# A gated MLP kernel: sums of the plain chunks kept in DRAM instead of in SBUF

## The chip, the cores and the metric

The kernel runs on one core of a Trainium2 chip. The metric is the device time of one execution in microseconds; each version is run several times and the median counts. The profile is of one further execution, which has a time of its own.

## What is computed

One transformer layer on 2048 tokens of width 576, in float32: layernorm, attention of 32 heads in which each token sees 8 tokens at steps of 2, an output projection with a residual, layernorm again, and a gated MLP with a hidden width of 4608.

```python
x = A_x
h = x + _A_ref(_layernorm(x), A_wqkv, A_wo)          # attention over 8 positions, then wo
g = einsum("bsd,df->bsf", layernorm(h), w_gate)
u = einsum("bsd,df->bsf", layernorm(h), w_up)
h2 = h + einsum("bsf,fd->bsd", sigmoid(g) * u, w_down)
```

## The kernel before

**Blocks and precision.** The tokens lie in four blocks of 512 (`BLOCKS`). Matrix products are made in float32 accuracy from halves: `split` (L103 to L105) has ScalarE write the rounded upper part of an operand (L104) and VectorE the remainder (L105), and three matmuls take the place of one. So each operand, whether a weight, an activation or a hidden value, costs one ScalarE and one VectorE instruction.

**Stages.** First come layernorm, the q, k and v projections and part of attention (to about 225 us). Then the MLP goes through its 4608 hidden columns in chunks of 128 (`F`, `NF` = 36), in a list of items (L1123) that is also the order of the program:

- twelve plain chunks (`NSTD` = 12) for block 0 (about 225 to 365 us),
- 24 paired chunks for blocks 0 and 1 together (to about 806 us),
- twelve plain chunks for block 1 (to about 950 us),
- 36 paired chunks for blocks 2 and 3 (to the end).

A paired chunk computes two blocks with seven products in place of eight (`pair`, L818); for that the inputs of its two blocks are combined into sums and differences (`sums`, L279 to L291: the rows L281 to L289) and split. A plain chunk (`single`, L783) needs one block only. While plain chunks of block 0 run on TensorE, attention and the output projection of block 1 run in between them (`under_first`, L1033); while plain chunks of block 1 run, the projections of blocks 2 and 3 do (`under_rest`, L1052). These steps in between are handed out at fixed places of a chunk (`bg_step`, L1086).

**Background steps that matter here.** Attention is VectorE's: products, reductions and sums of 128x2304 elements (L189 to L226). A finished group of heads goes out to DRAM by GpSimd's queue (L228, L230), and the projection loads it again by SyncE's queue (L707 in `paced`). It is transposed by TensorE (L146, L150), split (L105, L109), multiplied (L157 to L160), added to the residual by VectorE (L262) and normalised (`ln_j`, L118), where GpSimd computes one power (L126). Weights of a chunk are loaded by L702 into one of two buffers; a buffer is free when ScalarE and VectorE have split what it held.

**The down product.** Every two chunks there is a set of four units per block, one for each 128 tokens. A unit is `down_tile` (L859): twelve matmuls (L868) into a PSUM tile `dp`, of which there are two, and then its emptying, `add_tile` (L873): a copy by ScalarE (L876) or an addition to what lies in SBUF by VectorE (L878). Units stand in a list (`queue`, L1110) and are handed out at fixed places of a chunk (`units`, L1112).

In the paired chunks of blocks 0 and 1, `down_units` (L886) copies four units into a fresh `stage` tile with ScalarE, and `add_dram` (L883) adds the whole tile, 1152 KB, to `hacc[b]` in DRAM with one accumulating transfer of GpSimd's queue (L884). In the paired chunks of blocks 2 and 3, `down_seven` does the same with pieces of 576 and 288 KB (L936, L939). In the plain chunks, `down_std` (L895) keeps one `stage` tile through all six sets of a block: the first set is copied into it, the other five are added by VectorE, and after the sixth the tile is added to `hacc[b]` with one transfer. `hacc[b]` holds the residual from the projection before (L625, L973) and is sent to the output later (L1256).

**What sets the order.** The order of instructions on each engine is fixed when the kernel is built, from the order of the program, from priorities (`tc.high_priority`, the emptying of PSUM with `HC`, splits and projections mostly with `HI`) and from a cost model. On the chip each engine takes its queue in order and waits where an operand isn't there. GpSimd's transfers have the ordinary priority.

Of the kernel before, what the change touches and what calls it, by code (L numbers as in the profile page):

```python
# [18 lines left out]
ALU = mybir.AluOpType  # L19
# [4 lines left out]
D = 576  # L24
# [6 lines left out]
NS = 4  # L31
# [23 lines left out]
NSTD = 12  # L55
# [5 lines left out]
def kernel(ctx, tc, x, wqkv, wo, wmlp, out):  # L61
    nc = tc.nc
    dve, act, pool, pe, sp = nc.vector, nc.scalar, nc.gpsimd, nc.tensor, nc.sync
# [29 lines left out]
    hacc = [dr.tile([P, NS, D], F32, name=f"h{b}") for b in range(2)]  # L93
# [765 lines left out]
    def down_tile(seg, t, j):  # L859
        js = slice(j * P, (j + 1) * P)  # L860
        ps = gp.tile([P, 2, 512], F32, bufs=2, name="dp")
        k = 0
        n = 3 * len(seg) - 1
        for hid, d in seg:
            hh, hl = hid[t]
            for a, m in ((hh, 0), (hl, 0), (hh, 1)):
                for i in range(2):
                    pe.matmul(ps[:, i, :DH2], a[:, js], d[:, m, i * DH2:(i + 1) * DH2],  # L868
                              start=k == 0, stop=k == n)
                k += 1  # L870
        return ps[:, :, :DH2]

    def add_tile(hv, ps, copy):  # L873
        with tc.high_priority(HC):
            if copy:
                act.activation(hv, ps, AF.Copy)  # L876
            else:
                dve.tensor_tensor(hv, hv, ps, ALU.add)  # L878

    def halved(hs, j):  # L880
        return hs[:, j].rearrange("p (i n) -> p i n", i=2)

    def add_dram(b, hs):  # L883
        pool.dma_start(hacc[b], hs, accum_op=ALU.add, max_dma_last_dim=8 * D)  # L884
# [10 lines left out]
    def down_std(seg, b, n):  # L895
        if n == 0:
            tails[b] = st.tile([P, NS, D], F32, name="stage")
        hs = tails[b]
        for j in range(NS):
            add_tile(halved(hs, j), down_tile(seg, b, j), n == 0)  # L900
            if j == NS - 1 and n == NSTD // 2 - 1:
                add_dram(b, hs)
            yield

    def down_tail(seg, b, end):
# [220 lines left out]
    seg = []  # L1126
# [124 lines left out]
    for c, (kind, p, f) in enumerate(items):  # L1251
# [68 lines left out]
        if len(seg) == 2:  # L1320
            if by_seven and f == NF - NPL + 1:
                queue.append(load_tails())
            for b in blocks:
                queue.append(down_std(seg, b, f // 2) if kind == "std" else
                             down_tail(seg, b, f == NF - 1) if by_seven else down_units(seg, b))
            seg = []
# [44 lines left out]
```

## Time and profile before

| | |
|---|---|
| median of 3 runs | 1567.01 us (1566.04 to 1567.74) |
| profiled execution | 1568.13 us, of it 1566.4 us span |
| granted TensorE clock | 0.999 |
| TensorE, weight loads | 1542.5 us, 1373.7 us |
| VectorE | 1253.5 us |
| ScalarE | 874.0 us |
| GpSimd | 207.1 us |
| moved | 273.96 MB, 175 GB/s |

A busy time is the time in which the engine has an instruction of its own at work, and DMA issues count on GpSimd's row as its instructions. Matmuls overlap in a pipeline, so TensorE can be busy in the profile and yet be handed matmuls more slowly than it could take them; the pace at which matmuls start tells that. In rows of a timeline the columns are start, length, engine, line and operation, written tile and read tiles, and behind them, in brackets, the idle time of the engine ahead of the row and what ended it. Engines: PE is TensorE, PEld its weight loads, DVE VectorE, ACT ScalarE, POOL GpSimd, SP SyncE.

### The profile page before, as it was taken

The page shows a single profiled execution, that of the slowest core. Times are in us where ns is not written, and L with a number is a line of the kernel's source. Part 1 is how long each engine was busy: PE and PEld are TensorE (multiplying, and loading weights), DVE is VectorE, ACT ScalarE, POOL GpSimd, SP SyncE. Part 2 cuts the span into 40 slices and gives each one's busy share as a digit, 9 for nine tenths or more (in the row PEclk, how much of TensorE's full clock was granted, in tenths as well). Part 3 has the DMA queues.
Part 4 walks back from the last instruction along what each step waited for, and adds up shares of the span by engine and source line. Part 5 has one row for each costly group of instructions (what it writes and reads, how often), then busy time and mean ns, then how long its engine had stood idle before and what let it go on. Part 6 is the DMA issues. An engine that isn't in the chain of part 4 may idle for free.

```text
span 1566.4 us, 22385 instructions
## 1 busy us (share of the span) xinstructions
PE 1542.5 (98%) x8520; PEld 1373.7 (88%) x8520; DVE 1253.5 (80%) x1880; ACT 874.0 (56%) x1584; POOL 207.1 (13%) x252
## 2 busy tenths in 40 slices
PE   8999999999999999999999999999999999999998
PEld 7899888887888888888888888888888888888888
DVE  6998999969999999999526588866777776677754
ACT  6632245435656555666542355766677766677761
POOL 2300000011000110001101010112121121111212
PEclk9999999999999999999999999999999999999999
DMA  8646545266566776665683424898888889888984
GB/s 279 211 173 211 202 186 192 100 220 212 121 186 167 184 183 160 165 161 117 170 243 128 175 81 127 186 189 177 167 177 190 183 164 191 177 161 187 190 167 136
DMA packets 77148, 273.96 MB, mean 175 GB/s; under 512 B 8336, under 2 KB 14224, under 8 KB 76144
## 3 DMA queue, kind: packets, MB, share of 16 engines
q0 software_dynamic: 28192, 107.29, 37.4%
q1 hardware_dynamic: 41216, 145.11, 27.0%
q10 hardware_dynamic: 7632, 20.12, 3.4%
q8 instruction: 66, 1.08, 0.3%
q14 instruction: 42, 0.34, 0.1%
HBM read 143.98 MB, written 130.87 MB: 175 GB/s over the span
## 4 chain that ended last, share of the span: by engine, by line
PE 83%; DVE 8%; DMA 5%; ACT 1%; issue 1%; POOL 0%; ACTq 0%; SPq 0%; POOLq 0%; DVEq 0%
PE b L747 41%; PE dp L868 15%; PE dp L930 11%; PE b L754 8%; PE acc L157 4%; DMA wg<-in_wmlp_dram 2%; DVE pr L189 1%; DVE lg L193 1%; DVE pr L215 1%; PE b L157 1%; PE bgp L157 1%; DMA kw<-k 1%; DMA x<-tok 1%; DMA k<-ev 1%; DVE w L105 0%
## 5 line engine op out<-in xcount | busy, mean ns | idle before, releaser
L747 PE MATMUL b<-tl,w 128*128 128x512 f32 x1692 | 423.4, 392 | 1.6 <-ACT s L824 1.0
L747 PEld LDWEIGHTS b<-tl,w 128*128 128x128 f32 x1692 | 307.6, 188 | 59.7 <-ACT s L824 1.5
L747 PE MATMUL b<-th,w 128*128 128x512 f32 x1332 | 341.4, 391 | 0.4 <-DVE s L843 0.4
L747 PEld LDWEIGHTS b<-th,w 128*128 128x128 f32 x1332 | 246.0, 188 | 48.9 <-DVE s L843 0.8
L754 PE MATMUL b<-th,w 128*128 128x512 f32 x564 | 174.6, 390 | 0.0
L939 POOL DMA_DIRECT2D h<-ev x128 | 109.2, 853 | 455.9 <-ACT ev L936 451.0
L104 ACT ACTIVATE w<-wg 128x384 fp32r<-128x384 f32 (+1 forms) x186 | 111.0, 600 | 91.2 <-PE b L754 47.3
L157 PE MATMUL acc<-qw,th 128*128 128x432 f32 x512 | 154.3, 362 | 3.1 <-DVE th L109 2.3
L936 ACT ACTIVATE ev<-dp 128x576 f32<-128x576 f32 x224 | 139.0, 648 | 22.0 <-PE dp L930 22.0
L105 DVE TENSOR_TENSOR w<-wg,w 128x384 fp32r<-128x384 f32 (+1 forms) x186 | 120.9, 655 | 37.3 <-ACT w L104 37.1
L105 DVE TENSOR_TENSOR w<-tw,w 128x512 fp32r<-128x512 f32 x120 | 82.5, 688 | 79.6 <-ACT w L104 79.3
L754 PEld LDWEIGHTS b<-th,w 128*128 128x128 f32 x564 | 105.9, 188 | 22.5
L104 ACT ACTIVATE w<-tw 128x512 fp32r<-128x512 f32 x120 | 75.6, 630 | 83.4 <-PE b L747 82.3
L868 PE MATMUL dp<-d,h1h 128*128 128x288 f32 x640 | 118.8, 295 | 0.0
L868 PE MATMUL dp<-d,h0h 128*128 128x288 f32 x608 | 112.3, 295 | 0.0
L876 ACT ACTIVATE stage<-dp 128x576 f32<-128x576 f32 x104 | 66.9, 646 | 68.3 <-PE dp L868 68.1
L157 PEld LDWEIGHTS acc<-qw,th 128*128 128x128 f32 x512 | 96.7, 189 | 8.8 <-DVE th L109 3.4
L868 PEld LDWEIGHTS dp<-d,h1h 128*128 128x128 f32 x640 | 98.8, 189 | 3.0
L868 PEld LDWEIGHTS dp<-d,h0h 128*128 128x128 f32 x608 | 94.0, 189 | 3.5 <-DVE stage L878 0.3
L157 PE MATMUL acc<-qw,tl 128*128 128x432 f32 x256 | 92.8, 362 | 0.1
L189 DVE TENSOR_TENSOR pr<-kw,q 128x2304 f32<-128x2304 f32 x32 | 81.8, 2556 | 10.9 <-DMA kw<-k 10.7
L884 POOL DMA_DIRECT2D h<-stage x26 | 31.1, 1197 | 416.6 <-ACT stage L876 337.6
(323 smaller groups left out, 2971.6 us busy)
## 6 DMA issues: line engine op xcount, KB each, us to landing
h<-ev POOLq DMA_DIRECT2D x96, 576.0 KB, 7.1
wg<-in_wmlp_dram SPq DMA_DIRECT2D x47, 928.0 KB, 5.2
h<-stage POOLq DMA_DIRECT2D x26, 1152.0 KB, 11.7
wg<-in_wmlp_dram SPq DMA_DIRECT2D x36, 640.0 KB, 5.3
kw<-k SPq DMA_DIRECT2D x16, 792.0 KB, 5.1
vw<-v SPq DMA_DIRECT2D x16, 792.0 KB, 5.1
wd<-in_wmlp_dram SPq DMA_DIRECT2D x18, 576.0 KB, 8.1
h<-ev POOLq DMA_DIRECT2D x32, 288.0 KB, 5.1
```

The source lines that it names most:

```text
L104: act.activation(hi, src, AF.Copy)
L105: splits.append(dve.tensor_tensor(lo, src, f32(hi), ALU.subtract))
L157: pe.matmul(ps[:, :n], a[:, c, js], m[:, c], start=k == 0, stop=False)
L189: dve.tensor_tensor(pr, both(kw, u), q[:, us].unsqueeze(2).broadcast_to([P, 2, W, CG]), ALU.mult)
L747: pe.matmul(ps, wt[:, a, k0 + c], xx[:, m + c], start=first and k == 0, stop=k == 5, skip_group_check=True)
L754: pe.matmul(ps, wt[:, a, k0], xx[:, 4], start=False, stop=a == 1, skip_group_check=True)
L868: pe.matmul(ps[:, i, :DH2], a[:, js], d[:, m, i * DH2:(i + 1) * DH2], start=k == 0, stop=k == n)
L876: act.activation(hv, ps, AF.Copy)
L884: pool.dma_start(hacc[b], hs, accum_op=ALU.add, max_dma_last_dim=8 * D)
L930: pe.matmul(ps[:, i, :DH2], a[x][:, js], m[y], start=k in (0, 1, 3) and q == 0, stop=q == 2, skip_group_check=True)
L936: act.activation(hs[:, k % 2], ps[:, :, :DH2], AF.Copy)
L939: pool.dma_start(hsev[:, u, k0:k + 1], hs[:, :k + 1 - k0], accum_op=ALU.add, max_dma_last_dim=8 * D)
```

## The change

In `down_std` all six sets are copied by ScalarE, and each unit's row of the `stage` tile, 288 KB, is added to `hacc[b]` in DRAM right after its copy, by an accumulating transfer of GpSimd's queue. The VectorE addition and the one transfer behind the sixth set are gone. The `stage` tile stays the same through the six sets, so a row is written again in each of them.

```diff
         hs = tails[b]
         for j in range(NS):
-            add_tile(halved(hs, j), down_tile(seg, b, j), n == 0)
-            if j == NS - 1 and n == NSTD // 2 - 1:
-                add_dram(b, hs)
+            add_tile(halved(hs, j), down_tile(seg, b, j), True)
+            pool.dma_start(hacc[b][:, j], hs[:, j], accum_op=ALU.add, max_dma_last_dim=8 * D)
             yield
```

## Prediction

> **What bounds the kernel now.** I read the page first: its busy times, then the slices.
>
> ```profile
> span 1566.4 us, 22385 instructions
> ...
> PE 1542.5 (98%) x8520; PEld 1373.7 (88%) x8520; DVE 1253.5 (80%) x1880; ACT 874.0 (56%) x1584; POOL 207.1 (13%) x252
> ...
> DVE  6998999969999999999526588866777776677754
> ```
>
> TensorE is busy 98% of the span, so taking work off another engine is worth only what TensorE loses by waiting for it. VectorE has nines from about 120 us to 420 us: in the first plain stage it has no room, whatever its mean of 80% says. The view by windows tells how much there is to win in each stage (columns: stretch, its length, then busy time with the count of instructions of PE, PEld, DVE, ACT, POOL, then clock, DMA share, GB/s).
>
> ```profile
> 225.00:310.00 85.00, 84.69 (x453) 73.89 (x452) 80.92 (x97) 40.24 (x65) 0.71 (x1) 1.00 0.47 169
> 310.00:345.00 35.00, 33.73 (x222) 30.51 (x221) 24.41 (x56) 11.23 (x23) 5.30 (x9) 1.00 0.58 212
> 345.00:376.00 31.00, 30.08 (x160) 24.78 (x159) 28.17 (x40) 18.08 (x31) 7.36 (x11) 1.00 0.59 168
> 376.00:415.00 39.00, 37.58 (x194) 31.85 (x194) 35.73 (x50) 20.78 (x36) 1.23 (x1) 1.00 0.63 203
> 415.00:800.00 385.00, 385.00 (x2136) 341.86 (x2135) 347.56 (x438) 224.46 (x368) 33.90 (x32) 1.00 0.66 168
> 806.00:840.00 34.00, 32.11 (x193) 28.43 (x192) 18.65 (x32) 14.74 (x30) 1.20 (x1) 1.00 0.74 241
> 840.00:960.00 120.00, 118.89 (x721) 107.21 (x720) 83.79 (x160) 47.59 (x89) 12.62 (x17) 1.00 0.35 116
> ```
>
> The first plain stage and the turn into the pairs behind it (225 to 415) hold 3.9 us without a matmul (0.31 + 1.27 + 0.92 + 1.42). The second (806 to 960) holds 3.0 (1.89 + 1.11). That is 6.9 us to win. Between 415 and 800 there is none, though VectorE is at 90% and the DMA engines at 0.66 there: load alone costs nothing; only a late result does. So I looked for the places where TensorE waits for something on which VectorE's adds lie. These are rows of PE's timeline, after one row of the chain (start, length, line and count) which gives the pace of unhindered matmuls.
>
> ```profile
> 403.54 2.74 PE b L747 x12
> ```
>
> ```profile
> 319.77 0.65 PE L146 MATMUL b<-ident,oj 128*128 128x128 f32 x4 [0.45 <-DMA oj<-o]
> ...
> 364.24 1.60 PE L747 MATMUL b<-tl,w 128*128 128x512 f32 x5
> 366.28 3.23 PE L747 MATMUL b<-tl,w 128*128 128x512 f32 x11 [0.44 <-ACT tl L104]
> 369.34 0.61 PE L754 MATMUL b<-th,w 128*128 128x512 f32 x2
> ...
> 388.59 1.21 PE L747 MATMUL b<-tl,w 128*128 128x512 f32 x4 [1.03 <-ACT s L824]
> ...
> 881.51 0.33 PE L150 MATMUL bgp<-ident,oj 128*128 128x128 f32 x1 [1.11 <-DVE th L109]
> ```
>
> Twelve matmuls in 2.74 us make 0.228 us each. From 364.24 to 369.34 there are 16 of them in 5.10 us where 3.65 would do: 1.4 us lost, more than the 0.44 that is marked. The marked waits are 0.45 at 319.77, 1.03 at 388.59 and 1.11 at 881.51. Next the VectorE rows of the same places.
>
> ```profile
> 310.79 0.76 DVE L226 TENSOR_TENSOR kw<-kw 128x576 f32<-128x576 f32 x1
> ...
> 353.21 0.75 DVE L878 TENSOR_TENSOR stage<-stage,dp 128x576 f32<-128x576 f32 x1
> ...
> 358.62 1.41 DVE L878 TENSOR_TENSOR stage<-stage,dp 128x576 f32<-128x576 f32 x2
> ...
> 361.71 0.75 DVE L878 TENSOR_TENSOR stage<-stage,dp 128x576 f32<-128x576 f32 x1 [0.21 <-PE dp L868]
> ...
> 364.99 0.75 DVE L878 TENSOR_TENSOR stage<-stage,dp 128x576 f32<-128x576 f32 x1
> 365.65 1.22 DVE L105 TENSOR_TENSOR tl<-ar,tl 128x1024 fp32r<-128x1024 f32 x1
> ...
> 375.61 0.55 DVE L105 TENSOR_TENSOR w<-wg,w 128x384 fp32r<-128x384 f32 x1
> ...
> 880.38 0.76 DVE L878 TENSOR_TENSOR stage<-stage,dp 128x576 f32<-128x576 f32 x1
> 881.16 0.29 DVE L109 TENSOR_TENSOR th<-bgp,th 64x128 fp32r<-64x128 f32 x1
> ```
>
> **The change, part by part.** First what an add, a copy and a transfer cost.
>
> ```profile
> L878 DVE TENSOR_TENSOR stage<-stage,dp x40: 734/750/756, 259.8 to 953.0; 128x576 f32<-128x576 f32 x40
> ```
>
> ```profile
> L876 ACT ACTIVATE stage<-dp x104: 628/652/657, 240.8 to 824.5; 128x576 f32<-128x576 f32 x104
> ```
>
> ```profile
> L939 POOL DMA_DIRECT2D h<-ev x128: 852/852/906, 981.7 to 1519.6; - x128
> ...
> DMA to landing us min/median/max: 4.3/6.1/9.5
> ```
>
> ```profile
> h<-stage POOLq DMA_DIRECT2D x26, 1152.0 KB, 11.7
> ...
> h<-ev POOLq DMA_DIRECT2D x32, 288.0 KB, 5.1
> ```
>
> *Removed: 40 adds on VectorE,* 40 x 0.75 = 30 us, twenty in each plain stage. In the pair stages nothing changes. What it gives to TensorE, place by place:
>
> (a) At 319.77 the projection's input comes late. It left VectorE with L226 at 310.79, behind twelve adds of this stage (sets two to four), 12 x 0.67 = 8 us at the distance in which two adds follow each other (the 1.41 us of two, less 0.75). VectorE is 95% busy there (80.92 of 85), so most of the 8 us comes forward. All of the 0.45 goes: gain 0.4.
>
> (b) Between 353 and 365 VectorE has five adds (rows above) among the operand sums of the first pair, and 364.99 stands straight ahead of a split (365.65) for which TensorE loses its 1.4 us. Five adds away are 3.3 us earlier. What is late next is ScalarE's half of those splits, and ScalarE gets the five copies, 5 x 0.65 = 3.3 us. Its idle time there covers them (3.06 ahead of one row below, 2.17 ahead of the other); without that cover the gain would be lost again. I take 1.1 of the 1.4, bounds 0 and 1.4.
>
> ```profile
> 362.86 0.60 ACT L834 ACTIVATE s<-b 128x512 f32<-128x512 f32 x1 [3.06 <-PE b L747]
> ...
> 368.39 0.60 ACT L838 ACTIVATE s<-b 128x512 f32<-128x512 f32 x1 [2.17 <-PE b L747]
> ```
>
> (c) At 388.59 ScalarE was late since the weights of that chunk landed late: their load was issued at 376.19, right after VectorE had split the old contents (375.61), and took 10.6 us, the longest of the fourteen loads of this stretch (median 4.7).
>
> ```profile
> 376.19 0.33 SPq L702 DMA_DIRECT2D wg<-in_wmlp_dram  x1
> ```
>
> ```profile
> DMA to landing us min/median/max: 4.5/4.7/10.6
> ```
>
> In the old kernel the 1152 KB of sums were sent at 366.05, beside this rush (row below). In the new one three quarters of them are gone before, and VectorE frees the buffer a little sooner. I take 0.8 of 1.03, bounds 0 and 1.03.
>
> (d) At 881.16 a split waits behind the add at 880.38: 0.7 of the 1.11 goes.
>
> Together 0.4 + 1.1 + 0.8 + 0.7 = 3.0 us.
>
> *Added: 40 copies on ScalarE,* 26 us, thirteen in each stage. ScalarE is busy 40 of 85 us and 48 of 120 in the windows above, so they lie beside other work; each takes the place of an add in emptying the PSUM tile and is 0.1 us shorter. What queues behind a copy that waits for its matmuls is a weight split or a sigmoid. I take 0.3 us for all such places together, bounds 0 and 1.
>
> *Added: 48 accumulating transfers of 288 KB for two of 1152 KB.* GpSimd's issue: 46 more x 0.85 = 39 us on an engine with 0.71 us of work in the first 85 and 12.6 in the last 120. Beside it stand the layernorms' powers, the spills of attention and one load of operands:
>
> ```profile
> 311.85 0.71 POOL L228 DMA_DIRECT2D o<-kw  x1 [42.93 <-DVE kw L226]
> ...
> 347.35 0.59 POOL L1017 DMA_DIRECT2D ar<-x  x1 [1.46 <-PE dp L868]
> 366.05 1.25 POOL L884 DMA_DIRECT2D h<-stage  x1 [18.11 <-DVE stage L878]
> ```
>
> A power that finds an issue ahead of it comes 0.85 late at most, and the load at 347.35 by about as much; its data are used at about 357 (6.6 us to land), so nothing comes of it. Bytes: 48 x 288 - 2 x 1152 = 11,520 KB more, which raises the DMA share in the plain stages by some 0.2; the pair stage lost nothing at 0.66. I take 0 us, bounds 0 and 1.
>
> *Added wait:* a unit's copy overwrites a row of the one stage tile, so it must wait until the transfer of that row, sent one set earlier, is through. Copy, issue and landing are 0.65 + 0.85 + 5.1 = 6.6 us; the same row comes round after 11.8 us at the shortest (353.21 to 364.99). Cost 0, and rival two if landing is slow. Here the Trainium skill speaks against the change: its page "DMA: Bandwidth & Descriptors" (section "Measured") wants transfers of 1 MiB or more. The trace agrees in direction: four at 5.1 us are 20 us where one of 1152 KB is 11.7; by the page's fit (section "Anatomy of one DMA — SWDGE (gpsimd) path": 2.0 us and bytes over 436 GB/s) a 288 KB transfer would be an estimated 2.7 us, which no row of an accumulating transfer here shows. As no engine waits for landing in my sum, the rule leaves it unchanged.
>
> *Sum:* -3.0 + 0.3 = -2.7 us. Made against the profiled execution (1568.1 us, 1566.4 of them span) that is 1565.4; against the median of the runs, 1567.0, it is **1564.3 us**, 0.17% less. About 0.2%, 3.1 us, is what a measurement of this kernel can tell from no change.
>
> **The rivals.** *One, nothing comes of it:* the order on each engine is fixed when the kernel is built, and with other costs the tool may put the projection's matmuls elsewhere, so that TensorE waits elsewhere for as much. For it: of the 6.9 us most are chains from TensorE through VectorE back to TensorE. Against: (b) and (d) have the add itself ahead of the late split. Time 1567.0.
>
> *Two, the wait for the row replaces the add (slower):* GpSimd works in order, and its queue holds spills that wait 43 us for VectorE (row 311.85). Units' transfers that stand behind that spill go out only at about 313.4; the first lands at 319.3 after issue and 5.1 us, while ScalarE wants the row at about 316.4: 2.9 us in which ScalarE stands, its weight splits behind it. At the turn into the pairs the row has 11.8 us; if the landing takes 12 rather than 5.1, as beside the rush there (up to 9.5 in the row of the 128 issues, 11.7 for the big ones), the last copy is 1.7 us late and holds up the splits for which TensorE waits. It decides from a landing of about 10 us, or from one unit's transfer behind a spill. Price 4.6 with the gains lost: 1571.6. Against it: a wait of 43 us there says only that GpSimd had nothing else to do.
>
> *Three, more than I count:* all 6.9 us of TensorE's idle time go, as the whole projection runs earlier under a freed VectorE. For it: 95% and 91% of VectorE's time taken at 225 and 345. Against: the waits in 806 to 840, 1.89 us, have no add near. Time 1560.1.
>
> **How the numbers follow.** Forecast 0.43, with its own range from 1562.4 (all of the four waits, 4.0 us, a fifth of the 2.9 us by which they fall short of 6.9, and nothing paid) to 1566.5 (half a microsecond gained); rival one 0.15; rival two 0.24; rival three 0.18. Of the forecast's range 1.5 in 4.1 us lie beyond 3.1 us, so 0.16 of its 0.43 counts as faster: faster is 0.16 + 0.18 = 0.34, the same 0.27 + 0.15 = 0.42, slower 0.24. The range reaches from just inside rival three to just inside rival two, 1560.5 to 1571.0, and leaves out about 0.1 on each side.
>
> **What would show it.** L878 keeps only the sixteen adds of the tail, L876 has 144 copies, and a new issue line on GpSimd has 48. PE idle in the first plain stage falls from 3.9 to about 2, with no wait marked "ACT tl" or "DMA oj" there. Right for rival two: ScalarE waiting for a DMA on the stage tile, or a GpSimd issue of a unit right behind a spill. Wrong altogether: a loss that lies in the pair stages, where I count none, or a gain over 6.9 us.

## The result and the profile after

| | before | after |
|---|---|---|
| median of the runs | 1566.53 us (1565.97 to 1567.74, 4 runs) | 1585.2 us (1583.42 to 1586.59, 4 runs) |
| ratio | 1 | 1.0123, 95% interval 1.0108 to 1.0138 |
| profiled execution, its span | 1568.13 us, 1566.4 us | 1583.42 us, 1581.6 us |
| granted TensorE clock | 0.999 | 0.997 |

The change makes the kernel slower by 1.2%, some 19 us. In the experiments below, one run of the kernel with the change in block 1 alone, which had a clock of 0.851 and took 1688.40 us, is left out of its median. From the page after, the span, the busy times, the queue of GpSimd's transfers (packets, MB, share of the time of 16 DMA engines) and the new transfers (count, KB each, median us to landing):

```profile
span 1581.6 us, 22529 instructions
...
PE 1546.1 (98%) x8520; PEld 1377.8 (87%) x8520; DVE 1228.9 (78%) x1840; ACT 895.3 (57%) x1624; POOL 244.1 (15%) x298
...
q0 software_dynamic: 34560, 119.09, 42.1%
...
h<-stage POOLq DMA_DIRECT2D x48, 288.0 KB, 5.5
```

The engines did what the edit says: VectorE has 40 instructions and 25 us less, ScalarE 40 more and 21 us more, GpSimd 46 more and 37 us more. TensorE's 8520 matmuls are the same and are at work 3.6 us longer, so the other 11.6 us of the longer span are waiting. Where they lie is in the view by windows:

```profile
225.00:310.00 85.00, 80.72 (x427) 70.22 (x426) 72.42 (x83) 43.50 (x72) 15.08 (x18) 0.98 0.79 205
310.00:345.00 35.00, 29.14 (x189) 26.11 (x187) 19.77 (x50) 9.92 (x21) 5.63 (x9) 0.95 0.59 205
345.00:390.00 45.00, 41.03 (x216) 34.39 (x215) 36.96 (x48) 26.85 (x46) 12.17 (x16) 1.00 0.90 257
...
430.00:800.00 370.00, 370.00 (x2049) 328.63 (x2048) 332.12 (x421) 215.16 (x354) 32.51 (x31) 1.00 0.65 164
806.00:850.00 44.00, 39.01 (x218) 34.08 (x217) 17.05 (x29) 19.36 (x38) 6.38 (x7) 0.96 0.85 227
850.00:975.00 125.00, 123.80 (x751) 111.42 (x750) 76.06 (x149) 58.43 (x109) 26.75 (x34) 1.00 0.61 155
```

The first plain stage and the turn into the pairs now hold 4.28 + 5.86 + 3.97 = 14.1 us without a matmul, where the prediction's windows of before had 3.9; the second plain stage holds 4.99 + 1.20 = 6.2, where there were 3.0. That is 13.4 us more. It is more than the 11.6 us of the whole, since the opening of this execution happens to be idle 2.6 us less (9.8 and 12.5 of the first 225 us), which the change does not touch. In the pair stage between them TensorE is still never without a matmul. VectorE, which was to be relieved, is idle 12.6 of the first 85 us (it was idle 4.1), in part relief and in part waiting with the rest. The DMA share in those 85 us is 0.79 where it was 0.47.

The view of TensorE's waits from 225 to 400 us (what waited for what: us in total, times, longest) shows three large ones:

```profile
PE b L146 <- DMA oj<-o: 5.0, 1, 5.0
PE dp L868 <- ACT h0h L104: 3.9, 1, 3.9
PE b L747 <- ACT s L834: 2.0, 1, 2.0
```

The chain of waits from 255 to 320 us leads through the first two (start, length, what):

```profile
263.28 7.56 DMA wg<-in_wmlp_dram
...
271.51 0.63 ACT stage L876
...
274.15 2.47 DVE pr L189
276.62 0.61 DVE s L767
277.25 0.64 ACT h0h L104
277.93 0.54 PE dp L868 x2
...
305.24 6.33 DMA o<-kw
311.70 4.85 DMA oj<-o
316.59 1.11 PE b L146 x4
```

*The wait at 277.93.* A weight load takes 7.56 us to land. ScalarE stands 4.06 us at the split of those weights (row 270.87 below), and the next splits and the copy of a unit stand behind it in its queue. VectorE's half comes late in turn, and its order puts a 2.47 us product of attention ahead of the multiplication `s` (L767) that TensorE needs.

*The wait at 316.59.* VectorE finished the attention group early, but the spill of the result and its reload took 6.33 + 4.85 us.

*The third,* 2.0 us, ends at 389.16. The chain to it leads through two weight loads, which land 8.82 us after 369.44 and 6.27 us after 381.64.

The rows of ScalarE:

```profile
270.87 0.74 ACT L104 ACTIVATE w<-wg 128x640 fp32r<-128x640 f32 x1 [4.06 <-DMA wg<-in_wmlp_dram]
...
842.10 0.74 ACT L104 ACTIVATE w<-wg 128x640 fp32r<-128x640 f32 x1 [4.66 <-DMA wg<-in_wmlp_dram]
842.74 1.17 ACT L876 ACTIVATE stage<-dp 128x576 f32<-128x576 f32 x2
843.80 0.60 ACT L104 ACTIVATE th<-bgp 128x512 fp32r<-128x512 f32 x1
```

The last three show the same thing in the second plain stage: a weight split that waits 4.66 us, behind it two copies and then the split of the projection's input (L104, 843.80). TensorE waits 3.0 us for VectorE's half of that split (waits of TensorE from 800 to 990 us):

```profile
PE bgp L150 <- DVE tl L105: 3.0, 1, 3.0
```

In all four places a transfer that landed late stands behind the wait. How much later they land is in the rows of the lines that issue them, from 225 to 376 us. First the weight loads (L702) and the spills of attention (L228) of before:

```profile
DMA to landing us min/median/max: 4.5/4.6/9.3
```

```profile
DMA to landing us min/median/max: 2.8/3.0/3.2
```

The same two of after:

```profile
DMA to landing us min/median/max: 4.6/6.1/8.8
```

```profile
DMA to landing us min/median/max: 5.4/6.2/6.9
```

The two spills take twice as long, and half of the eleven weight loads now take 6.1 us or more, with the same bytes and the same queues as before. The sum of ScalarE's waits for weights hardly rose in that stretch, from 12.8 us to 14.0 (10.7 ahead of `w` and 3.3 ahead of `d`). What is new is that one of them reaches TensorE, with VectorE's product in between.

### The profile page after: what moved, and what is told of

The parts are those of the page before. It is cut to its first block, busy times and chain, and to the rows that moved or that the text cites. A ratio compares the mean times of both kernels' runs of the same rounds, so it can differ in the third digit from the quotient of the medians.

```text
span 1581.6 us, 22529 instructions
## 1 busy us (share of the span) xinstructions
PE 1546.1 (98%) x8520; PEld 1377.8 (87%) x8520; DVE 1228.9 (78%) x1840; ACT 895.3 (57%) x1624; POOL 244.1 (15%) x298
## 3 DMA queue, kind: packets, MB, share of 16 engines
q0 software_dynamic: 34560, 119.09, 42.1%
## 4 chain that ended last, share of the span: by engine, by line
PE 78%; DVE 8%; DMA 8%; ACT 2%; issue 2%; POOL 1%; SPq 0%; ACTq 0%; POOLq 0%; DVEq 0%
PE b L747 39%; PE dp L868 13%; PE dp L929 11%; PE b L754 7%; DMA wg<-in_wmlp_dram 4%; PE acc L157 4%; DVE lg L193 1%; DVE pr L189 1%; PE b L157 1%; DVE pr L215 1%; PE bgp L157 1%; DMA x<-tok 1%; DVE w L105 1%; DMA h<-in_x_dram 1%; DMA ar<-x 1%
## 5 line engine op out<-in xcount | busy, mean ns | idle before, releaser
L747 PE MATMUL b<-tl,w 128*128 128x512 f32 x1692 | 424.0, 393 | 3.1 <-ACT s L834 2.0
L747 PEld LDWEIGHTS b<-tl,w 128*128 128x128 f32 x1692 | 309.0, 189 | 60.6 <-ACT s L834 2.6
L747 PE MATMUL b<-th,w 128*128 128x512 f32 x1332 | 343.5, 393 | 0.8 <-DVE s L767 0.8
L747 PEld LDWEIGHTS b<-th,w 128*128 128x128 f32 x1332 | 247.1, 189 | 49.4 <-DVE s L767 1.2
L105 DVE TENSOR_TENSOR w<-wg,w 128x384 fp32r<-128x384 f32 (+1 forms) x186 | 121.1, 654 | 52.7 <-ACT w L104 52.2
L104 ACT ACTIVATE w<-wg 128x384 fp32r<-128x384 f32 (+1 forms) x186 | 110.7, 600 | 80.5 <-PE b L754 40.5
L105 DVE TENSOR_TENSOR w<-tw,w 128x512 fp32r<-128x512 f32 x120 | 82.5, 687 | 87.7 <-ACT w L104 87.6
L876 ACT ACTIVATE stage<-dp 128x576 f32<-128x576 f32 x144 | 92.7, 645 | 83.5 <-PE dp L868 81.8
L104 ACT ACTIVATE w<-tw 128x512 fp32r<-128x512 f32 x120 | 75.7, 631 | 95.1 <-PE b L747 85.4
L868 PE MATMUL dp<-d,h1h 128*128 128x288 f32 x640 | 118.7, 295 | 0.0
L868 PE MATMUL dp<-d,h0h 128*128 128x288 f32 x608 | 112.8, 295 | 4.8 <-ACT h0h L104 3.9
L868 PEld LDWEIGHTS dp<-d,h0h 128*128 128x128 f32 x608 | 94.0, 189 | 8.5 <-ACT h0h L104 4.1
L868 PEld LDWEIGHTS dp<-d,h1h 128*128 128x128 f32 x640 | 98.6, 189 | 2.9
L189 DVE TENSOR_TENSOR pr<-kw,q 128x2304 f32<-128x2304 f32 x32 | 81.7, 2552 | 7.1 <-DMA kw<-k 6.9
L215 DVE TENSOR_TENSOR pr<-vw,lg 128x2304 f32<-128x2304 f32 x32 | 81.8, 2555 | 0.6
```

The costliest lines, as they stand in the source:

```text
L104: act.activation(hi, src, AF.Copy)
L105: splits.append(dve.tensor_tensor(lo, src, f32(hi), ALU.subtract))
L189: dve.tensor_tensor(pr, both(kw, u), q[:, us].unsqueeze(2).broadcast_to([P, 2, W, CG]), ALU.mult)
L215: dve.tensor_tensor(pr.rearrange("p j w (h d) -> p j w h d", d=DH), both(vw, u).rearrange("p j w (h d) -> p j w h d", d=DH), lg[:, us].uns ...
L747: pe.matmul(ps, wt[:, a, k0 + c], xx[:, m + c], start=first and k == 0, stop=k == 5, skip_group_check=True)
```

## The experiments

Two theories stood against each other. *Traffic:* the 11.8 MB of accumulating transfers make other transfers land later, and the plain stages have no lead over their loads. *Order:* with copies for adds, the tool that fixes the order of instructions puts TensorE's work elsewhere, and TensorE waits there. Some expectations name a third, *both:* an order that is tight and fails only when transfers are late. A loss below is the ratio less 1, by 1566.5 us; ratios come from runs taken side by side and need not be the quotient of two medians.

### Traffic without the change, the change without traffic

`e1_traffic_only` leaves the kernel before as it is and adds the transfers, from an operand tile into a spare tile in DRAM:

```diff
             add_tile(halved(hs, j), down_tile(seg, b, j), n == 0)
+            src = X["a01" if b == 0 else "a11"].rearrange("p c n -> p (c n)")[:, :D]
+            pool.dma_start(hx[b][:, j], f32(src), accum_op=ALU.add, max_dma_last_dim=8 * D)
```

> The kernel before, with VectorE's adds and the order of every engine's instructions but GpSimd's as they were, plus the 48 accumulating transfers of 288 KB: they read a tile of operands that nothing overwrites and add into a spare buffer in DRAM. Theory traffic (the added transfers slow the loads and spills that others wait for): most of the loss, 1578 to 1585 us. Theory order (the loss comes from the new fixed order of matmuls and splits, which VectorE's missing adds brought about): 1565.5 to 1568. Theory both (a tight order that only fails when transfers are late): 1567 to 1573.

Measured: 1583.73 us (1582.86 to 1590.26, 4 runs), ratio 1.0115, interval 1.0092 to 1.0138. The order of instructions on TensorE, VectorE, ScalarE and SyncE is the one of before, to the instruction. From its windows, and its waits of ScalarE (225 to 376 us) and TensorE (225 to 430 us; the added lines move L104 to L105 and L868 to L869):

```profile
225.00:310.00 85.00, 73.36 (x360) 62.24 (x359) 64.72 (x79) 32.88 (x57) 17.83 (x21) 0.94 0.82 234
```

```profile
ACT w L105 <- DMA wg<-in_wmlp_dram: 34.4, 10, 6.7
```

```profile
PE dp L869 <- ACT h0h L105: 7.0, 3, 5.9
```

So transfers alone, in the old order, can cost as much as the whole change. ScalarE waits 34.4 us ahead of `w` and another 9.2 ahead of `d`, all for weights, and TensorE waits for what stands behind these splits.

That the two losses agree is in part luck. The spare transfers wait for no copy, so they go out earlier and closer together than those of the change, and they are 14.2 MB, since the two old ones of 1152 KB stay. Their issues (L903 is the added line):

```profile
L903 POOL DMA_DIRECT2D hx<-th x24: 850/859/1900, 214.5 to 275.7; - x24
...
L903 POOL DMA_DIRECT2D hx<-th x20: 856/864/1892, 366.1 to 416.1; - x20
```

The 24 of block 0 go out in 61 us, where the changed kernel takes 145 (238.5 to 383.8). Of block 1's, 20 go out in the turn into the pairs and only four near the second plain stage, at 955 us. The loss follows the first 24: from 225 to 310 us TensorE is without a matmul for 11.6 us (0.3 before) at a clock of 0.94, while from 806 to 975 us it is so for 1.9 us (3.0 before). The 20 in the turn cost nothing, though the DMA share reads 1.06 for much of that time:

```profile
390.00:430.00 40.00, 39.96 (x205) 34.00 (x205) 37.06 (x54) 21.89 (x38) 13.27 (x16) 1.00 1.06 292
```

`e2_copy_only` is the change without the transfers of the first five sets:

```diff
-            pool.dma_start(hacc[b][:, j], hs[:, j], accum_op=ALU.add, max_dma_last_dim=8 * D)
+            if n == NSTD // 2 - 1:
+                pool.dma_start(hacc[b][:, j], hs[:, j], accum_op=ALU.add, max_dma_last_dim=8 * D)
```

> The changed kernel with ScalarE's 48 copies and, but for a few places, its order, with the transfers left out but for those of the last set of each block (so the sums of the first five sets are missing from the output). Theory traffic: the gain that was forecast appears, 1562 to 1566 us. Theory order: 1578 to 1585. Theory both: 1566 to 1574.

Measured: 1569.45 us (1565.46 to 1576.11, 10 runs), ratio 1.0014, interval 0.9998 to 1.0031. Some ten to twenty instructions on each of TensorE, VectorE and ScalarE stand elsewhere than in the kernel after. The loss is all but gone with the transfers: the order alone is refuted as its cause. By what was expected the time lies with theory both and not with traffic, since the gain did not appear. Whether the new order makes the same traffic dearer is not shown, as no run sends the change's transfers at their own times in the old order. And what the prediction counted as gain isn't there: 2.7 us less would be a ratio of 0.9983. Its window and its waits of TensorE (both 225 to 430 us) tell why:

```profile
225.00:430.00 205.00, 200.75 (x1111) 175.18 (x1110) 178.92 (x245) 111.73 (x190) 18.77 (x26) 1.00 0.57 187
```

```profile
PE b L747 <- ACT s L838: 1.6, 1, 1.6
PE dp L868 <- ACT h0h L104: 1.2, 1, 1.2
...
PE b L146 <- DMA oj<-o: 0.6, 1, 0.6
```

VectorE has 26 of 205 us to spare, yet TensorE is without a matmul for 4.25 us, as much as before (3.9 from 225 to 415), at ScalarE and still at the reload. In the second plain stage, from 806 to 975 us, it is so for 2.3 us where it was 3.0. Its profiled execution happens to be the fastest of the ten and as fast as forecast (1565.46); the median isn't.

### How much traffic, and of what kind

`e3_plain_write` is the change with the first five sets' transfers as plain writes to a spare tile:

```diff
-            pool.dma_start(hacc[b][:, j], hs[:, j], accum_op=ALU.add, max_dma_last_dim=8 * D)
+            if n == NSTD // 2 - 1:
+                pool.dma_start(hacc[b][:, j], hs[:, j], accum_op=ALU.add, max_dma_last_dim=8 * D)
+            else:
+                pool.dma_start(hx[b][:, j], hs[:, j], max_dma_last_dim=8 * D)
```

> The changed kernel with the same order on every engine, the transfers of the first five sets written to a spare buffer in DRAM without adding (their sums are missing from the output). If it is the reading and adding in DRAM that makes the transfers costly: 1567 to 1575 us. If it is that there are transfers at all: 1582 to 1586. Theory order: 1582 to 1586 as well.

Measured: 1575.4 us (1571.82 to 1577.3, 5 runs), ratio 1.0044, interval 1.0028 to 1.0061. Every engine's order is that of the changed kernel, to the instruction, and so is the number of transfers. So some 12 of its 19 us hang on what accumulating transfers do on the DMA engines beyond plain ones.

`e5_one_per_set` is e1 with one transfer of 1152 KB for each set in place of four of 288 KB:

```diff
+            src = f32(X["a01" if b == 0 else "a11"].rearrange("p c n -> p (c n)"))
+            if j == NS - 1:
+                pool.dma_start(hx[b].rearrange("p j d -> p (j d)"), src[:, :NS * D], accum_op=ALU.add,
+                               max_dma_last_dim=8 * D)
```

> The kernel before in its own order, with the same added bytes as in the run with traffic alone, but as one accumulating transfer of 1152 KB per set in place of four of 288 KB. A big one lands in 11.3 us, a small one in 5.5. If each transfer costs by its number and its rows of 2304 bytes: about half the loss, 1574 to 1577 us. If the bytes cost: 1581 to 1586. If a long transfer at one time delays one weight load by more than it spares the others: over 1586.

Measured: 1582.43 us (1578.94 to 1588.17, 4 runs), ratio 1.0105, interval 1.0065 to 1.0146.

`e6_half_units` is e1 with the transfers of units 0 and 2 alone:

```diff
+            src = f32(X["a01" if b == 0 else "a11"].rearrange("p c n -> p (c n)"))
+            if j % 2 == 0:
+                pool.dma_start(hx[b][:, j], src[:, :D], accum_op=ALU.add, max_dma_last_dim=8 * D)
```

> The kernel before in its own order, with accumulating transfers of 288 KB for every second unit: half the traffic. If the loss goes with the bytes: 1574 to 1577 us. If there is room for some traffic and the loss begins beyond it: under 1571.

Measured: 1576.22 us (1572.1 to 1580.71, 6 runs), ratio 1.0067, interval 1.0045 to 1.0088.

The time that the packets of GpSimd's queue took is its share on the page times the span, over all 16 DMA engines. Beside the loss:

| kernel | queue's share, span | its time | more than before | loss |
|---|---|---|---|---|
| before | 37.4% of 1566.4 | 586 us | | |
| after | 42.1% of 1581.6 | 666 | 80 | 19 us |
| e1, 48 accumulating of 288 KB | 42.0% of 1581.1 | 664 | 78 | 18 |
| e5, 12 accumulating of 1152 KB | 41.6% of 1581.3 | 658 | 72 | 16 |
| e6, 24 accumulating of 288 KB | 39.7% of 1574.9 | 625 | 39 | 10.5 |
| e3, plain writes | 39.2% of 1575.3 | 617 | 32 | 7 |
| e2, none but the last set | 37.6% of 1563.5 | 588 | 2 | 2 |

Half the transfers of e1 cost about half, plain writes of the change's bytes less than half, and no gain from batching can be told: the intervals of e1 and e5 lie over each other and leave some 7 us either way. Where transfers were added, the loss is 0.22 to 0.27 of the added time. GpSimd's issues are not what costs: e3 has as many as the changed kernel and loses 12 us less, e5 has 36 fewer than e1 and loses about as much. Nor do they slow VectorE: its product L189 takes 2556 ns on average before and 2552 after.

That the ratio is so even says less than it seems to. It is a mean over places where added transfers cost much and places where they cost nothing (e1 above; e5 and e6 send theirs at about the same times), and four transfers at one place are worth 8 us or nothing (e10 and e11 below). As to larger transfers, which the prediction weighed: at the same bytes the queue's time is 6 us less in e5 than in e1, and the kernel's time is not told apart.

### One block alone

`e4_block0_only` makes the change in the first plain stage alone, `e12_block1_only` in the second alone (the diff of the first):

```diff
-            add_tile(halved(hs, j), down_tile(seg, b, j), n == 0)
-            if j == NS - 1 and n == NSTD // 2 - 1:
+            add_tile(halved(hs, j), down_tile(seg, b, j), n == 0 or b == 0)
+            if b == 0:
+                pool.dma_start(hacc[b][:, j], hs[:, j], accum_op=ALU.add, max_dma_last_dim=8 * D)
+            elif j == NS - 1 and n == NSTD // 2 - 1:
                 add_dram(b, hs)
```

> The change in the first plain stage (block 0) alone, block 1 as before. From the pace of matmuls the first stage lost 12 us more than before and the second 5. If the two add up: 1578 to 1581 us. If the first stage's loss is in truth handed on to the second: 1584 or more.

> The change in the second plain stage alone. Block 0 alone took the whole loss (1586.3), while the pace of the matmuls put 5 us of it into the second stage. If the stages are independent: 1570 to 1573 us. If the second stage lost only since it was handed a late start: 1566 to 1568.

Measured: e4 1586.34 us (1583.0 to 1588.89, 4 runs), ratio 1.0121, interval 1.0101 to 1.0141. e12 1573.51 us (1571.73 to 1575.43, 3 runs), ratio 1.0044, interval 1.0028 to 1.0061. By these the first stage costs 19 us and the second 7, and both together 19, so they do not add up. The traces come closer. TensorE is without a matmul for 16.0 us from 225 to 430 us in e4 and 14.1 in the changed kernel (3.9 before), and for 6.7 us from 806 to 975 us in e12 and 6.2 in the changed kernel (3.0 before). And e4's profiled execution was 34 matmuls behind before the changed stage began, by an event that has nothing to do with the change (last section). Whether its other executions were so too is not on record, and the rest stays open. Both stages cost something, the first more, in which attention's spills and reloads run beside the weights.

### Which of the late landings decides

Most of the waiting of ScalarE was for weights, which have two buffers. A third buffer gives some loads more lead; every third load goes into `stage` space that is idle in that part:

```diff
-    def load_gu(f, eng=sp, n=WC):
-        ws = gw.tile([P, WC], F32, bufs=2, name="wg")
+    def load_gu(f, eng=sp, n=WC, more=False):
+        if more:
+            ws = st.tile([P, NS, D], F32, name="stage").rearrange("p j d -> p (j d)")[:, :WC]
+        else:
+            ws = gw.tile([P, WC], F32, bufs=2, name="wg")
...
-            wg = load_gu(items[c + 2][2], n=WC if c + 2 < NF + NSTD else GU)
+            wg = load_gu(items[c + 2][2], n=WC if c + 2 < NF + NSTD else GU, more=c + 2 in (4, 7, 10))
```

It stands in e7 (on the kernel after), e8 (on the kernel before) and e9 (on e1).

> The changed kernel, with every third of the weight loads of the first plain stage put into the stage buffer that lies idle there, so that a load may start one chunk sooner; all transfers and all bytes stay. If the loss is weight loads that have too little lead (theory late loads): all but the one wait of about 5 us on the projection's input goes, 1570 to 1575 us. If the transfers slow something else (the queue of GpSimd, VectorE's ports): 1582 to 1587.

> The kernel before with the same third buffer and no added traffic. ScalarE waits 12.8 us in all for weight loads in the first plain stage, of which little reaches the matmuls. Theory late loads: 1564 to 1567 us, at most the idle time of that stage (3.9 us) faster.

> The order of the kernel before with the third weight buffer, plus the same 48 accumulating transfers of spare data as in the run with traffic alone (1583.7 us). There ScalarE waited 34.4 us for weights in the first plain stage, and the matmuls waited behind it. Theory late loads: with a chunk more of lead that loss goes, 1572 to 1576 us (the third buffer without traffic took 1572.7). If the traffic costs whatever the lead of the weights is: 1582 to 1588.

Measured: e7 1585.07 us (1582.93 to 1587.21, 4 runs), ratio 1.0119, interval 1.0093 to 1.0145. e8 1572.7 us (1567.73 to 1575.08, 10 runs), ratio 1.0036, interval 1.0018 to 1.0053. e9 1586.56 us (1586.1 to 1587.66, 4 runs), ratio 1.0128, interval 1.0113 to 1.0144. The third buffer wins nothing in any of them, and what theory late loads expected of the three did not come. In e7 it did what it was for (waits of ScalarE from 225 to 376 us, then of TensorE from 225 to 430 us; L868 is L871 here, L747 is L750):

```profile
ACT d L104 <- DMA stage<-in_wmlp_dram: 4.0, 1, 4.0
...
ACT w L104 <- DMA wg<-in_wmlp_dram: 0.6, 1, 0.6
```

```profile
PE b L146 <- DMA oj<-o: 5.4, 1, 5.4
PE b L750 <- ACT s L837: 2.1, 1, 2.1
PE dp L871 <- ACT h0h L104: 2.0, 1, 2.0
```

With one more of 0.6 us ahead of `d`, ScalarE's waits for weights fell from 14.0 us in all to 5.2, and TensorE's wait behind them from 3.9 to 2.0. But the wait for the reload stayed, the one at `s` stayed, and some twenty instructions on each of TensorE, VectorE and ScalarE changed places. In e9 the extra load, sent amid the rush, is itself the one that lands late:

```profile
248.31 0.68 ACT L105 ACTIVATE d<-stage 128x576 fp32r<-128x576 f32 x1 [11.61 <-DMA stage<-in_wmlp_dram]
```

ScalarE stands 11.61 us for it. A buffer more lets a load start sooner, but it did not make this one land in time.

`e10_no_transfers_set4` goes at the other place: the kernel after without the four transfers of block 0's fourth set, which stand beside the spill and the reload.

```diff
-            pool.dma_start(hacc[b][:, j], hs[:, j], accum_op=ALU.add, max_dma_last_dim=8 * D)
+            if b == 1 or n != 3:
+                pool.dma_start(hacc[b][:, j], hs[:, j], accum_op=ALU.add, max_dma_last_dim=8 * D)
```

> The changed kernel in its own order, the four transfers of block 0's fourth set left out (these sums are missing from the output); they fall at the spill of attention's last group and its reload, for which the matmuls waited 5.0 us. Theory spill (the transfers beside it double its landing): the 5.0 us and the 1.7 us of half clock behind it go, 1577 to 1580 us. Against it, if only the mean traffic counts: one twelfth of the loss less, 1583.5.

Measured: 1585.4 us (1580.99 to 1588.89, 4 runs), ratio 1.0118, interval 1.0098 to 1.0139. Its waits of TensorE (225 to 430 us):

```profile
PE dp L868 <- ACT h0h L104: 5.1, 1, 5.1
PE b L146 <- DMA oj<-o: 2.7, 1, 2.7
PE b L747 <- ACT s L834: 2.6, 1, 2.6
```

The reload costs 2.7 us where it cost 5.0, and the other two waits are 1.2 and 0.6 longer. What one place gives back, less than 3 us, is taken elsewhere; the 1577 to 1580 us of theory spill did not come. `e11_third_buffer_no_set4` has both edits:

> Both of these in the changed kernel: third weight buffer, and no transfers of block 0's fourth set. Theory that late weights and the late reload are all of block 0's loss: 1571 to 1576 us. If a third thing is as large: over 1579.

Measured: 1577.09 us (1574.95 to 1579.89, 4 runs), ratio 1.0073, interval 1.0056 to 1.009: 8 us less than the kernel after, and as much less than e7, whose order it has to the instruction. No wait of TensorE for the reload is left. Its window:

```profile
225.00:310.00 85.00, 82.72 (x444) 71.70 (x443) 74.54 (x88) 45.91 (x78) 12.47 (x15) 1.00 0.81 230
```

The DMA share is as high as in the kernel after (0.81 and 0.79), yet TensorE is without a matmul for 2.3 us and not 4.3. The four transfers that are left out are 4 of 48, by the table some 2 us of 19 at most. So the share as such does not cost; late results at these two places do. Serving one of them wins nothing (e7, e10), serving both wins 8 us. What is left, 11 us, is about what block 1 (e12, 7 us) and the third buffer by itself (e8, 6 us) cost. `e13_block0_third_no_set4` is the same with block 1 as before:

> The change in block 0 alone, with the third weight buffer and without the transfers of block 0's fourth set (these sums are missing from the output); block 1 as before. With both blocks changed the same two took the time to 1577.1 us, and block 1 alone cost 7.4. If what is left there is block 1's: 1568 to 1572 us. If a third thing in block 0 is as large as the two: 1575 or more.

Measured: 1572.56 us (1568.76 to 1576.54, 7 runs), ratio 1.0036, interval 1.0021 to 1.0051. That is the time of the third buffer by itself (e8, 1.0036), so with both edits block 0's remaining five sets of transfers cost nothing that can be told, to some 3.5 us, and they gain nothing either. The orders of the two kernels differ, so this is close to a comparison of like with like, but not quite one. Why the third buffer costs some 6 us in the old kernel was not settled. No version beat the kernel before.

## Why the prediction was wrong

The sign was wrong, and the time lies outside the range.

*The step that failed* is the cost of the added transfers: "raises the DMA share in the plain stages by some 0.2; the pair stage lost nothing at 0.66. I take 0 us, bounds 0 and 1." With the order kept, accumulating transfers in place of plain writes are worth 12 us (the changed kernel against e3); with only a few places moved, having the transfers or not is worth 17 (against e2). The share was forecast well: from 225 to 430 us it rose by 0.18, from 0.53 to 0.71 (by 0.32 in the first 85 us). The error was to take the pair stage as proof that a share costs nothing. "Load alone costs nothing; only a late result does" holds (e11, at 0.81); what was not asked is which results would now be late. The trace of before could have been asked, by ScalarE's waits for weights; first from 225 to 376 us, then in the pair stage from 415 to 800:

```profile
ACT w L104 <- DMA wg<-in_wmlp_dram: 12.8, 7, 3.6
```

```profile
ACT w L104 <- DMA wg<-in_wmlp_dram: 3.3, 4, 1.6
```

In 151 us of the plain stage there are seven such waits, 12.8 us, with eleven loads sent; in 385 us of pairs there are four, 3.3 us, with 22 loads sent, though these land later (5.6 us median, 4.6 in the plain stage). In the plain stage most loads are waited for as it is; in the pair stage most have lead. The nearest row was not the nearest case.

*The gains (a) to (d), 3.0 us together:* none can be told in the times of e2, which has the relief without the traffic. (a) VectorE's L226 came forward from 310.79 to 303.53:

```profile
303.53 0.75 DVE L226 TENSOR_TENSOR kw<-kw 128x576 f32<-128x576 f32 x1
```

Of these 7.3 us 3.4 are the quicker opening of this execution: the L226 of the group that ends at the start of the stage stands at 219.31 and not 222.66. The relief of the stage itself is 3.9 us with the traffic, and 9.6 without it (e2, 221.60 to 300.09, where before took 222.66 to 310.79), so the 8 us that were worked out are about right for the adds alone. But spill and reload, which the step did not count, took 8.2 us before (311.55 to 319.77) and 12.3 after (304.28 to 316.59). TensorE, whose order had been moved ahead with VectorE's, waits 5.0 us there and not 0.45. Even in e2 it waits 0.6 us there, at 309.94, some 10 us sooner than before: that is what *rival one* said of the gains, a new order in which TensorE waits for as much. *Rival three,* that all of the idle time goes, is refuted by the same run. (b) and (c) sit in the turn into the pairs, which now holds 4.0 us without a matmul from 345 to 390 (2.3 before); (c) counted on less traffic there, and the DMA share rose from 0.65 to 0.90. (d) in block 1 gave way to 3.0 us behind a late weight split; in e2's trace the second stage is idle 0.7 us less, which is (d)'s size. Of the signs that were named, idle time in the first plain stage was to fall from 3.9 to about 2 with no wait marked "DMA oj"; it is 14.1, and that wait is the largest; the one marked "ACT tl" did go.

*The copies,* "0.3 us, bounds 0 and 1": they queue as was said, and a weight split that waits holds them up, not the reverse. e2 has them and costs about 2 us (-0.3 to 4.9 by its interval) with the gains lost, so this term is not shown wrong, nor is it separated from the gains.

*The wait for the stage row,* 0: right. By the view of L876, ScalarE's 144 copies wait for matmuls (81.8 us in 67 places) and never for a transfer.

*Rival two* named the right side with the wrong mechanism: no row was overwritten late, and no unit's transfer stood long behind a spill. What it had right is the picture of ScalarE standing with its weight splits behind it; what holds it is the weights' own load. *Prices:* a copy at 651 ns and an issue at 849 ns (forecast 652 and 852), a landing at 5.5 us median (5.1), were right; the sum had no term for what they do to other transfers.

*A reading:* VectorE's slices do not hold nines from about 120 to 420 us. The slice from 313 to 352 us is a six, and the row of 310 to 345 us has VectorE busy for 24.4 of 35 us, so it had room in part of the first plain stage. No term of the sum rests on this.

## What to carry to other kernels

Before moving work from an engine to the DMA engines, ask in the stage concerned whether its loads have lead: if an engine already waits for landings there, added traffic can be dear, here 19 us for 80 us of added DMA engine time, by way of a few late landings and not byte by byte. A stage that carries the same load without loss proves nothing for one whose loads have less lead. And a chain that ends in a spill and a reload is not shortened by an earlier result alone; the two landings count with it. An experiment that adds traffic alone has to send it when the change does, which is to be read from its trace.

## What the runs showed of the hardware

*An accumulating transfer is dear.* The same 11.8 MB took 80 us of the DMA engines' time as accumulating transfers (after) and 32 us as plain writes (e3), 2.5 times as much. In e1 14.2 MB of them took 78 us, which is twice as much for each MB as in e3.

*A stall costs more than its length.* Two stretches of the kernel after, 4 us each, just behind its waits of 3.9 and 5.0 us, by the view by windows (the last columns are clock, DMA share and GB/s), and matmuls ahead of and behind the first:

```profile
278.00:282.00 4.00, 4.00 (x12) 3.17 (x13) 3.29 (x4) 0.78 (x2) 0.00 (x0) 0.57 0.67 238
316.00:320.00 4.00, 3.41 (x13) 3.00 (x14) 0.69 (x1) 1.15 (x3) 0.00 (x0) 0.57 1.05 412
```

```profile
269.92 1.52 PE L747 MATMUL b<-tl,w 128*128 128x512 f32 x6
...
278.30 2.61 PE L747 MATMUL b<-tl,w 128*128 128x512 f32 x6
```

Six matmuls take 2.61 us where six took 1.52: the granted clock is about half for some 3.4 us after each wait (0.57 over 4 us), which adds some 1.7 us to it. The wait of 3.0 us in the second plain stage is followed by the same (0.57 from 845 to 849 us). The Trainium skill, "TensorE: Matmul & The Clock Gate" (Part 1), has the clock go to half after an idle window of about 3.4 us and back after as long a busy one; these rows agree as to the length of the half clock. The wait can be shorter than that window: in e6 half clock follows waits of 2.4 us (0.57 from 412 to 416 us) and 2.1 us (0.60 from 836 to 840 us), while 2.0 us at 836.15 in the kernel after left the clock whole.

*The same event sets executions apart.* In some it comes in the opening, which the change does not touch and where TensorE's order is the same in all these kernels. The windows up to 225 us, first of the kernel after, then of e4:

```profile
0.00:225.00 225.00, 215.16 (x1158) 202.72 (x1159) 202.73 (x270) 96.60 (x226) 26.30 (x50) 1.00 0.60 211
```

```profile
0.00:225.00 225.00, 210.86 (x1124) 197.72 (x1125) 196.44 (x262) 91.69 (x218) 26.34 (x49) 0.98 0.58 199
```

The clock of e4 is lower, and 34 fewer matmuls are done by 225 us. From 180 to 188 us TensorE is at work for 2.6 us in e4 and 6.4 in the kernel after, and e4's clock is 0.61 and then 0.53 in the two stretches of 4 us from 184. At 0.19 us for one (215.16 us for 1158) the 34 matmuls are some 6 us. The profiled execution of e4 is 5.5 us slower than that of the kernel after (1588.89 and 1583.42 us), though it pays in one stage alone. What brings the event about in one execution and not in another was not tried.
